# FFT mixing and a ReGLU layer on one core: compute only the distinct token columns, and store them in ranges of 16 or 32 rows

## The chip, the core and the metric

The kernel runs on one core of one Trainium2 chip. The core has five engines with instruction streams of their own: TensorE (PE in the profile, its weight loads as PEld), VectorE (DVE), ScalarE (ACT), GpSimd (POOL) and SyncE (SP), which here only issues DMAs. SBUF is the on-chip memory, PSUM the memory that matmuls write. The metric is the device time of one execution in microseconds; the time before is the median of nine runs.

## What is computed

For 8 batches of 3008 tokens with 256 features, the reference takes the real part of a two-dimensional FFT over tokens and features, and sends the result through a gated layer of width 1536:

```python
X = np.fft.fft(x, axis=1)          # x: (8, 3008, 256)
X = np.fft.fft(X, axis=2)
x = X.real.astype(np.float32).reshape(24064, 256)
gate = np.maximum(x @ w_gate, 0.0)
val = x @ w_val
out = (gate * val @ w_out).astype(np.float32)
```

The input is real. So the transform at token S-r is that of token r with the sign of one half of its parts turned. Tokens 1 to 1503 have a mirror at 1505 to 3007; tokens 0 and S/2 = 1504 are their own. That makes 1505 distinct token columns in a batch.

## The kernel before

The token transform is split as 94 x 32: a token is r = ka + 94*kb with ka from 0 to 93 and kb from 0 to 31. Only ka from 0 to 47 is computed, in three blocks (`blk` 0, 1, 2) of 512 columns. A block has four groups (g) of 128 columns, and a group has four runs (u) of 32: ka = 12*u + 4*blk + g, and kb runs inside. 3 x 512 = 1536 columns, 31 more than are distinct.

The start-up builds sine tables and folds the features' transform into the weights: `wc` and `ws` for the two parts, and `wm`, which is `ws` times -2 (its row 0 is zero). Then come 288 steps (8 batches x 3 blocks x 12 slices `f` of the width). In each step, on 512 columns:

- `gate` (L467): two matmuls into PSUM `G` (L473, L474), ACT's ReLU into `gs` (L475). In blocks 0 and 2 POOL sets 32 mirrored columns of `h` to zero (L480).
- `mirror_gate` (L482): one more matmul adds `wm` and turns `G` into the mirror's gate (L485); ACT's ReLU makes `gm` (L488). It is on 480 columns in blocks 0 and 2: those of ka = 0 and ka = 47 are left out, and the zeros stand for them.
- `value` (L490): two matmuls into `V` (L495, L497), and DVE multiplies `gs` and `V` into the direct half of `h` (L499).
- `mirror_value` (L515): in a split step DVE makes the mirror's value from `V` in two operations (`even` L505, then L519), and POOL multiplies it with `gm` into the mirrored half of `h` (L511). In an unsplit step a third matmul (L523) makes it instead. `split` (L463) is false for the first 18 steps, then in one of 6 steps up to step 48, and in one of 12 after that.

The mirrored half is written with kb reversed within each run of 32.

Twelve steps after a block's first step its output begins: `out_piece` (L534) is called twice a step and issues four matmuls each time (L546), `h` as the weights and `wo` with 256 columns streaming through, 12 to a group of 128 tokens. Two groups share a PSUM tile `po` (two of them take turns); ACT copies it to `os` (L555); `store` (L568) issues four DMAs of 32 rows, one for each u, on SP. In the last block's mirrored half each group is copied by DVE (L551) and stored at once by `store_last` (L559), with SP and ACT as issuers.

Between these steps a hand-written plan places the next batches' work: loading x and folding it (POOL), the transform's first stage (L164), a shuffle through DRAM (L182, L188), `rotate`, and the second stage, `stage2` (L199, matmuls at L206), which writes `pq`, whose imaginary row 0 goes through DRAM (`Nd`) and comes back in all partitions as `nb`. All the HBM transfers of this but the gather of `xh` are issued on SP, in the order of the plan, in one queue with the stores.

The order of each engine's instructions is fixed when the program is built. So are the completion counters (semaphores) of the DMAs of SP and ACT: there are eight, handed out in turn in the order in which the DMAs of both are placed, and a DMA waits until the one that had its counter before has landed.

Of the kernel before, what the change touches and what calls it, by code (L numbers as in the profile page):

```python
# [14 lines left out]
ALU = mybir.AluOpType  # L15
ACTF = mybir.ActivationFunctionType
# [27 lines left out]
def kernel(ctx: ExitStack, tc, x, w_gate, w_val, w_out, out):  # L44
# [154 lines left out]
    def stage2(b, blk, cs, evac):  # L199
        if cs == 0:  # L200
            pqt[b, blk] = pqp.tile([128, 2, 512], BF16, tag="pq", name="pq")
            nbt[b, blk] = pqp.tile([128, 512], BF16, tag="nb", name="nb")
        t4, pq = t4t[b], pqt[b, blk]
        ps = bank(b, "ps2")
        for g in range(4):
            nc.tensor.matmul(ps[:, g * 128:(g + 1) * 128], lhsT=t4[:, 4 * blk + g, cs * H:(cs + 1) * H],  # L206
                             rhs=m2[:, cs, :], start=True, stop=True)
        if evac == "act":
            nc.scalar.copy(pq[:, cs, :], ps[:])
        else:  # L210
# [73 lines left out]
    with tc.tile_pool(name="sp", bufs=1, space=SB) as sp:  # L284
        dve, pl = nc.vector, nc.gpsimd
# [31 lines left out]
        ps = psd.tile([128, 512], F32, tag="d", name="psk")  # L317
        for k in range(WARM):
# [4 lines left out]
                allow_small_or_imprecise_dtypes=True)  # L323

        def product(eng, lo, hi):
# [6 lines left out]
                allow_small_or_imprecise_dtypes=True)  # L332
# [47 lines left out]
        for blk in range(NBLK):  # L380
# [1 line left out]
        load_w(2)  # L382

        kbi = sp.tile([128, 4, NB], F32, tag="kbi")
        pl.iota(kbi[:], pattern=[[0, 4], [1, NB]], base=0, channel_multiplier=0, allow_small_or_imprecise_dtypes=True)
        ui = sp.tile([128, 4, NB], F32, tag="ui")
        pl.iota(ui[:], pattern=[[1, 4], [0, NB]], base=0, channel_multiplier=0, allow_small_or_imprecise_dtypes=True)
        di = sp.tile([128, 4, 2, 16], F32, tag="di")
# [1 line left out]
                allow_small_or_imprecise_dtypes=True)  # L390
# [64 lines left out]
    steps = [(b, blk, f) for b in range(B) for blk in range(NBLK) for f in range(NF)]  # L455
    ht = {}

    def mirrored(t):

        blk = steps[t][1]  # L460
        return slice(NB if blk == 0 else 0, 512 - NB if blk == NBLK - 1 else 512)

    def split(t):  # L463

        return 18 <= t < len(steps) and t % (6 if t < 48 else 12) != 5

    def gate(t):  # L467
        b, blk, f = steps[t]
        pq, fs = pqt[b, blk], slice(f * 128, (f + 1) * 128)
        e = ht[t] = {"h": hp.tile([128, 2, 512], BF16, tag="h", name="h"),  # L470
                     "G": psg.tile([128, 512], F32, tag="g", name="G"),
                     "gs": gp.tile([128, 512], F32, tag="gs", name="gs")}
        nc.tensor.matmul(e["G"][:], lhsT=wc[0][:, fs], rhs=pq[:, 0, :], start=True, stop=False)  # L473
        nc.tensor.matmul(e["G"][:], lhsT=ws[0][:, fs], rhs=pq[:, 1, :], start=False, stop=True)  # L474
        nc.scalar.activation(e["gs"][:], e["G"][:], ACTF.Relu)  # L475
        cols = mirrored(t)
        if cols.stop - cols.start < 512:

            lo = 0 if cols.start else cols.stop
            nc.gpsimd.memset(e["h"][:, 1, lo:lo + NB], 0.0)  # L480

    def mirror_gate(t):  # L482
        b, blk, f = steps[t]
        e, cols = ht[t], mirrored(t)
        nc.tensor.matmul(e["G"][:, cols], lhsT=wm[0][:, f * 128:(f + 1) * 128], rhs=pqt[b, blk][:, 1, cols],  # L485
                         start=False, stop=True, skip_group_check=True)
        e["gm"] = ep.tile([128, 512], F32, tag="gm", name="gm")
        nc.scalar.activation(e["gm"][:, cols], e["G"][:, cols], ACTF.Relu)  # L488

    def value(t, part):  # L490
        b, blk, f = steps[t]
        e, pq, fs = ht[t], pqt[b, blk], slice(f * 128, (f + 1) * 128)
        if part == 0:
            e["V"] = psv.tile([128, 512], F32, tag="v", name="V")
            nc.tensor.matmul(e["V"][:], lhsT=wc[1][:, fs], rhs=pq[:, 0, :], start=True, stop=split(t))  # L495
        else:
            nc.tensor.matmul(e["V"][:], lhsT=ws[1][:, fs], rhs=pq[:, 1, :], start=False, stop=True,  # L497
                             skip_group_check=split(t))
            nc.vector.tensor_tensor(e["h"][:, 0, :], e["gs"][:], e["V"][:], op=ALU.mult)  # L499

    def even(t):
        b, blk, f = steps[t]
# [5 lines left out]
    def mirror_h(t, eng, val):  # L508

        e, cols = ht[t], mirrored(t)  # L510
        eng.tensor_tensor(free(e["h"][:], 512 + cols.start + NB - 1, [NB, (cols.stop - cols.start) // NB], [-1, NB]),  # L511
                          e["gm"][:, cols].rearrange("p (a k) -> p a k", k=NB),
                          val[:, cols].rearrange("p (a k) -> p a k", k=NB), op=ALU.mult)

    def mirror_value(t):  # L515
        b, blk, f = steps[t]
# [17 lines left out]
    def out_piece(t, half):  # L534

        b, blk, f = steps[t]
        for k in range(8 * f + 4 * half, 8 * f + 4 * half + 4):
            gi, ff = divmod(k, NF)
            sg, s = divmod(gi, 4)
            g = 3 - s if sg else s  # L540
            if s == 0 and ff == 0:
                state["os"] = op.tile([128, 4, D], F32, tag="os", name="os")
            if s % 2 == 0 and ff == 0:
                state["po"] = pso.tile([128, 2, D], F32, tag="o", name="po")
            po, os_ = state["po"], state["os"]
            nc.tensor.matmul(po[:, s % 2, :], lhsT=ht[t - f + ff]["h"][:, sg, g * 128:(g + 1) * 128],  # L546
                             rhs=wo[:, ff, :], start=(ff == 0), stop=(ff == NF - 1))
            if ff < NF - 1:
                continue
            if t - f == len(steps) - NF and sg == 1:  # L550
                nc.vector.tensor_copy(os_[:, s:s + 1, :], po[:, s % 2:s % 2 + 1, :])  # L551
                store_last(b, blk, os_, s)
                continue
            if s % 2 == 1:
                nc.scalar.copy(os_[:, s - 1:s + 1, :], po[:])  # L555
            if s == 3:
                store(b, blk, sg, os_)

    def store_last(b, blk, os_, s):  # L559

        for u in range(4):
            ka = NKA * u + 4 * blk
            if s == 0 and ka + 3 == 47:
                continue
            (nc.sync if u % 2 or s < 2 else nc.scalar).dma_start(
                out=view(out, (b * S + NA - ka - 3 + s) * D, [[NA * D, NB], [1, D]]), in_=os_[32 * u:32 * u + 32, s, :])

    def store(b, blk, sg, os_):  # L568
        for u in range(4):
            ka = NKA * u + 4 * blk  # L570
            src = os_[32 * u:32 * u + 32].rearrange("p g d -> p (g d)")
            if sg == 0:
                nc.sync.dma_start(out=view(out, (b * S + ka) * D, [[NA * D, NB], [1, 4 * D]]), in_=src)
                continue

            lo = 1 if ka + 3 == 47 else 0
            hi = 3 if ka == 0 else 4
            row = b * S + NA - ka - 3 + lo
            nc.sync.dma_start(out=view(out, row * D, [[NA * D, NB], [1, (hi - lo) * D]]),
                              in_=src[:, lo * D:hi * D])  # L580

    extra = {}

# [29 lines left out]
    n = len(steps)  # L613
# [56 lines left out]
```

## Time and profile before

| | us |
|---|---|
| median of 9 runs (649.84 to 652.48) | 650.58 |
| the profiled execution | 650.94 |
| its span on the core | 649.2 |
| PE busy (4170 matmuls) | 625.5 |
| weight loads (PEld) | 408.6 |
| DVE busy | 565.9 |
| POOL busy | 509.1 |
| ACT busy | 425.0 |
| 192 POOL memsets of `h`, L480 | 22.8 |
| 94 output copies on ACT, L555 | 55.1 |

The costliest groups are the output matmuls (L546), POOL's mirror product (L511) and the seven operations of a step on ACT and DVE. The columns are: line, engine, operation, tiles and shapes, count; then busy us and mean ns of one; then idle us of the engine just before them, and who ended most of it.

```profile
L511 POOL TENSOR_TENSOR h<-gm,E 128x480 bf16<-128x480 f32 (+1 forms) x251 | 308.2, 1228 | 92.5 <-DVE E L519 66.7
L546 PE MATMUL po<-wo,h 128*128 128x256 bf16 x2304 | 337.2, 272 | 2.8 <-DVE os L551 1.1
L499 DVE TENSOR_TENSOR h<-gs,V 128x512 bf16<-128x512 f32 x288 | 195.8, 687 | 17.6 <-ACT gm L488 12.0
L475 ACT ACTIVATE gs<-G 128x512 f32<-128x512 f32 x288 | 171.5, 595 | 0.8 <-PE G L474 0.8
```

Such a mean is the time from an instruction's start to its end. Instructions overlap, so the distance between two starts can be shorter; busy time counts each moment once.

### The profile page before, as it was taken

The page shows a single profiled execution, that of the slowest core. Times are in us where ns is not written, and L with a number is a line of the kernel's source. Part 1 is how long each engine was busy: PE and PEld are TensorE (multiplying, and loading weights), DVE is VectorE, ACT ScalarE, POOL GpSimd, SP SyncE. Part 2 cuts the span into 40 slices and gives each one's busy share as a digit, 9 for nine tenths or more (in the row PEclk, how much of TensorE's full clock was granted, in tenths as well). Part 3 has the DMA queues.
Part 4 walks back from the last instruction along what each step waited for, and adds up shares of the span by engine and source line. Part 5 has one row for each costly group of instructions (what it writes and reads, how often), then busy time and mean ns, then how long its engine had stood idle before and what let it go on. Part 6 is the DMA issues. An engine that isn't in the chain of part 4 may idle for free.

```text
span 649.2 us, 12804 instructions
## 1 busy us (share of the span) xinstructions
PE 625.5 (96%) x4170; PEld 408.6 (63%) x4246; DVE 565.9 (87%) x889; ACT 425.0 (65%) x813; POOL 509.1 (78%) x716
## 2 busy tenths in 40 slices
PE   6888999999999999999999999999999999999995
PEld 3424666666666666666666666666666666666664
DVE  9857688889999998989989998998988988989991
ACT  5366676776666667676676666766666767766660
POOL 9649469968998699968998699967999666666660
PEclk9599999999999999999999999999999999999999
DMA  9792473295134651295324852285322142212113
GB/s 246 226 229 50 126 192 82 58 217 177 40 82 115 148 161 42 50 188 156 81 66 112 175 142 60 50 172 149 102 50 73 31 131 73 50 34 64 32 40 88
DMA packets 32823, 70.77 MB, mean 109 GB/s; under 512 B 4650, under 2 KB 22146, under 8 KB 30754
## 3 DMA queue, kind: packets, MB, share of 16 engines
q1 hardware_dynamic: 30228, 58.03, 34.2%
q0 software_dynamic: 2336, 11.80, 9.0%
q8 instruction: 33, 0.54, 0.4%
q14 instruction: 34, 0.28, 0.1%
q10 hardware_dynamic: 192, 0.13, 0.1%
HBM read 39.77 MB, written 30.96 MB: 109 GB/s over the span
## 4 chain that ended last, share of the span: by engine, by line
PE 87%; DVE 5%; POOL 4%; issue 2%; ACT 1%; DVEq 0%; POOLq 0%; ACTq 0%
PE po L546 38%; PE V L497 9%; PE G L474 9%; PE G L485 8%; PE V L495 8%; PE G L473 8%; PE ps L164 2%; POOL eo L132 2%; DVE E L505 2%; PE ps L206 2%; PE psw L263 2%; DVE h L499 1%; PE V L523 1%; DVE E L519 1%; POOL h L511 1%
## 5 line engine op out<-in xcount | busy, mean ns | idle before, releaser
L511 POOL TENSOR_TENSOR h<-gm,E 128x480 bf16<-128x480 f32 (+1 forms) x251 | 308.2, 1228 | 92.5 <-DVE E L519 66.7
L546 PE MATMUL po<-wo,h 128*128 128x256 bf16 x2304 | 337.2, 272 | 2.8 <-DVE os L551 1.1
L546 PEld LDWEIGHTS <-h 128*128 128x128 bf16 x2304 | 222.8, 98 | 90.9 <-issue 2.8
L488 ACT ACTIVATE gm<-G 128x480 f32<-128x480 f32 (+1 forms) x288 | 167.5, 582 | 126.7 <-PE G L485 113.3
L499 DVE TENSOR_TENSOR h<-gs,V 128x512 bf16<-128x512 f32 x288 | 195.8, 687 | 17.6 <-ACT gm L488 12.0
L505 DVE SCALAR_TENSOR_TENSOR E<-nb,af,V 128x480 f32<-128x480 bf16 (+1 forms) x245 | 177.7, 725 | 22.4 <-PE V L495 12.4
L475 ACT ACTIVATE gs<-G 128x512 f32<-128x512 f32 x288 | 171.5, 595 | 0.8 <-PE G L474 0.8
L519 DVE SCALAR_TENSOR_TENSOR E<-E,V 128x480 f32<-128x480 f32 (+1 forms) x245 | 161.3, 658 | 0.0
L497 PE MATMUL V<-pq,ws 128*128 128x512 bf16 x287 | 108.7, 379 | 1.6 <-DVE E L505 1.1
L485 PE MATMUL G<-pq,wm 128*128 128x480 bf16 (+1 forms) x288 | 106.7, 370 | 2.2 <-ACT gs L475 2.2
L474 PE MATMUL G<-pq,ws 128*128 128x512 bf16 x281 | 106.5, 379 | 2.2 <-DVE pq L211 0.4
L495 PE MATMUL V<-pq,wc 128*128 128x512 bf16 x255 | 96.6, 379 | 0.0
L473 PE MATMUL G<-pq,wc 128*128 128x512 bf16 x253 | 95.9, 379 | 0.1
L555 ACT COPY os<-po 128x512 f32<-128x512 f32 x94 | 55.1, 586 | 60.2 <-PE po L546 60.2
L104 POOL TENSOR_TENSOR eo<-xl 94x254 bf16<-94x254 f32 (+2 forms) x100 | 74.7, 751 | 0.4
L101 POOL TENSOR_TENSOR xl<-xl,xh 94x510 f32<-94x510 f32 (+2 forms) x50 | 66.0, 1319 | 3.9
L497 PEld LDWEIGHTS <-ws 128*128 128x128 bf16 x288 | 28.2, 98 | 33.7
L474 PEld LDWEIGHTS <-ws 128*128 128x128 bf16 x288 | 28.2, 98 | 31.5 <-issue 0.2
L511 DVE TENSOR_TENSOR h<-gm,V 128x480 bf16<-128x480 f32 (+1 forms) x37 | 24.6, 665 | 22.7 <-ACT gm L488 17.1
L174 ACT CAST t<-ps 96x512 bf16<-96x512 f32 x63 | 36.9, 585 | 5.8 <-PE ps L162 5.4
L495 PEld LDWEIGHTS <-wc 128*128 128x128 bf16 x288 | 28.1, 98 | 10.5 <-issue 3.7
L485 PEld LDWEIGHTS <-wm 128*128 128x128 bf16 x288 | 28.2, 98 | 7.6 <-issue 4.1
(108 smaller groups left out, 349.1 us busy)
## 6 DMA issues: line engine op xcount, KB each, us to landing
out_dram<-os SPq DMA_DIRECT2D x173, 128.0 KB
xl<-in_x_dram SPq DMA_DIRECT2D x7, 1360.0 KB
Td<-t SPq DMA_DIRECT2D x7, 768.0 KB
t<-Td SPq DMA_DIRECT2D x7, 768.0 KB
nb<-Nd SPq DMA_DIRECT2D x24, 128.0 KB
xl<-in_x_dram SPq DMA_DIRECT2D x7, 238.0 KB
xl<-in_x_dram SPq DMA_DIRECT2D x4, 384.0 KB
xh<-in_x_dram SPq DMA_DIRECT2D x4, 384.0 KB
```

The source lines that it names most:

```text
L473: nc.tensor.matmul(e["G"][:], lhsT=wc[0][:, fs], rhs=pq[:, 0, :], start=True, stop=False)
L474: nc.tensor.matmul(e["G"][:], lhsT=ws[0][:, fs], rhs=pq[:, 1, :], start=False, stop=True)
L475: nc.scalar.activation(e["gs"][:], e["G"][:], ACTF.Relu)
L485: nc.tensor.matmul(e["G"][:, cols], lhsT=wm[0][:, f * 128:(f + 1) * 128], rhs=pqt[b, blk][:, 1, cols], start=False, stop=True, skip_group_ ...
L488: nc.scalar.activation(e["gm"][:, cols], e["G"][:, cols], ACTF.Relu)
L495: nc.tensor.matmul(e["V"][:], lhsT=wc[1][:, fs], rhs=pq[:, 0, :], start=True, stop=split(t))
L497: nc.tensor.matmul(e["V"][:], lhsT=ws[1][:, fs], rhs=pq[:, 1, :], start=False, stop=True, skip_group_check=split(t))
L499: nc.vector.tensor_tensor(e["h"][:, 0, :], e["gs"][:], e["V"][:], op=ALU.mult)
L505: nc.vector.scalar_tensor_tensor(e["E"][:, cols], nbt[b, blk][:, cols], af[:, f:f + 1], e["V"][:, cols], op0=ALU.mult, op1=ALU.add)
L511: eng.tensor_tensor(free(e["h"][:], 512 + cols.start + NB - 1, [NB, (cols.stop - cols.start) // NB], [-1, NB]), e["gm"][:, cols].rearrange ...
L519: nc.vector.scalar_tensor_tensor(e["E"][:, cols], e["E"][:, cols], 2.0, e["V"][:, cols], op0=ALU.mult, op1=ALU.subtract)
L546: nc.tensor.matmul(po[:, s % 2, :], lhsT=ht[t - f + ff]["h"][:, sg, g * 128:(g + 1) * 128], rhs=wo[:, ff, :], start=(ff == 0), stop=(ff == ...
```

## The change

`mirrored` and the new `direct` set the columns. In block 0 the first 16 columns fall away, in block 2 the last 15 or 16: direct products run on 496, 512 and 497 columns in the three blocks, mirrored ones on 496, 512 and 496. The run ka = 0 is turned by half (the iota `kbi` starts at NB/2 there), so that what falls away lies at the block's edge. Column 496 of the third block is token S/2, made by one extra one-column matmul in `stage2` for each half.

The mirrored half of `h` is now written fully reversed from its first column on, both halves begin at column 0, and the zeroing memset is gone. The last output group of an edge block therefore has 113 or 112 tokens (`m`), and its copy on ACT is done group by group.

`store` works out from `rows` which rows of `os` belong to consecutive output rows, and issues one DMA for each such range: 16 or 32 rows, with one of 15 rows in block 0 and the single row of token S/2. The very last half is stored group by group in the same way, each group with a `po` of its own; in its last group SP and ACT take turns. `store_last` is gone. `value` takes the columns of `direct` in the same way as `gate` in the diff, for both matmuls and the product.

```diff
@@ stage2
+        if blk == NBLK - 1:
+            nc.tensor.matmul(ps[:, 496:497], lhsT=t4[:, 0, cs * H:(cs + 1) * H], rhs=m2[:, cs, 0:1], start=True, stop=True)
@@ tables
-        pl.iota(kbi[:], pattern=[[0, 4], [1, NB]], base=0, channel_multiplier=0, allow_small_or_imprecise_dtypes=True)
+        pl.iota(kbi[:, 0, :], pattern=[[1, NB]], base=NB // 2, channel_multiplier=0,
+                allow_small_or_imprecise_dtypes=True)
+        pl.iota(kbi[:, 1:4, :], pattern=[[0, 3], [1, NB]], base=0, channel_multiplier=0, allow_small_or_imprecise_dtypes=True)
@@ columns
+    LO, HI = NB // 2, 512 - NB // 2
     def mirrored(t):
-        return slice(NB if blk == 0 else 0, 512 - NB if blk == NBLK - 1 else 512)
+        return slice(LO if blk == 0 else 0, HI if blk == NBLK - 1 else 512)
+    def direct(t):
+        return slice(LO if blk == 0 else 0, HI + 1 if blk == NBLK - 1 else 512)
@@ gate
-        nc.tensor.matmul(e["G"][:], lhsT=wc[0][:, fs], rhs=pq[:, 0, :], start=True, stop=False)
-        nc.tensor.matmul(e["G"][:], lhsT=ws[0][:, fs], rhs=pq[:, 1, :], start=False, stop=True)
-        nc.scalar.activation(e["gs"][:], e["G"][:], ACTF.Relu)
-        cols = mirrored(t)
-        if cols.stop - cols.start < 512:
-            lo = 0 if cols.start else cols.stop
-            nc.gpsimd.memset(e["h"][:, 1, lo:lo + NB], 0.0)
+        ds = direct(t)
+        nc.tensor.matmul(e["G"][:, ds], lhsT=wc[0][:, fs], rhs=pq[:, 0, ds], start=True, stop=False)
+        nc.tensor.matmul(e["G"][:, ds], lhsT=ws[0][:, fs], rhs=pq[:, 1, ds], start=False, stop=True)
+        nc.scalar.activation(e["gs"][:, ds], e["G"][:, ds], ACTF.Relu)
@@ mirror_h
-        eng.tensor_tensor(free(e["h"][:], 512 + cols.start + NB - 1, [NB, (cols.stop - cols.start) // NB], [-1, NB]),
-                          e["gm"][:, cols].rearrange("p (a k) -> p a k", k=NB),
-                          val[:, cols].rearrange("p (a k) -> p a k", k=NB), op=ALU.mult)
+        n = cols.stop - cols.start
+        eng.tensor_tensor(free(e["h"][:], 512 + n - 1, [-1, n]), e["gm"][:, cols], val[:, cols], op=ALU.mult)
@@ out_piece
-            if s % 2 == 0 and ff == 0:
+            if (g % 2 == 0 or last) and ff == 0:
                 state["po"] = pso.tile([128, 2, D], F32, tag="o", name="po")
-            nc.tensor.matmul(po[:, s % 2, :], lhsT=ht[t - f + ff]["h"][:, sg, g * 128:(g + 1) * 128],
+            nc.tensor.matmul(po[0:m, i, :], lhsT=ht[t - f + ff]["h"][:, sg, g * 128:g * 128 + m],
                              rhs=wo[:, ff, :], start=(ff == 0), stop=(ff == NF - 1))
-            if t - f == len(steps) - NF and sg == 1:
-                nc.vector.tensor_copy(os_[:, s:s + 1, :], po[:, s % 2:s % 2 + 1, :])
-                store_last(b, blk, os_, s)
+            if last:
+                nc.vector.tensor_copy(os_[0:m, g:g + 1, :], po[0:m, 0:1, :])
+                store(b, blk, sg, os_, g, g + 1, (nc.sync, nc.scalar) if g == 3 else (nc.sync,))
                 continue
-            if s % 2 == 1:
-                nc.scalar.copy(os_[:, s - 1:s + 1, :], po[:])
-            if s == 3:
-                store(b, blk, sg, os_)
+            if m < 128:
+                nc.scalar.copy(os_[:, g - 1, :], po[:, 0, :])
+                nc.scalar.copy(os_[0:m, g, :], po[0:m, 1, :])
+            elif g % 2 == 1:
+                nc.scalar.copy(os_[:, g - 1:g + 1, :], po[:])
+            if g == 3:
+                store(b, blk, sg, os_, 0, 4, (nc.sync,))
@@ store
+        for k, (p, n, ga, ng, ra) in enumerate(parts):
+            queues[k % len(queues)].dma_start(
+                out=view(out, ra * D, [[NA * D, n], [1, ng * D]]),
+                in_=os_[p:p + n, ga:ga + ng, :].rearrange("p g d -> p (g d)"))
+        if blk == NBLK - 1 and sg == 0:
+            nc.sync.dma_start(out=view(out, (b * S + S // 2) * D, [[D, 1], [1, D]]), in_=os_[HI % 128:HI % 128 + 1, 3, :])
```

In the built programs SP issues 199 stores before and 287 after, ACT 4 and 2. The last group alone has 15 before (11 on SP) and 23 after (21 on SP).

More of the change, by code (lines that the diff above doesn't have):

```diff
@@ L456 @@
     ht = {}
+    LO, HI = NB // 2, 512 - NB // 2
     def mirrored(t):
         blk = steps[t][1]
-        return slice(NB if blk == 0 else 0, 512 - NB if blk == NBLK - 1 else 512)
+        return slice(LO if blk == 0 else 0, HI if blk == NBLK - 1 else 512)
+    def direct(t):
+        blk = steps[t][1]
+        return slice(LO if blk == 0 else 0, HI + 1 if blk == NBLK - 1 else 512)
     def split(t):
@@ L492, in value @@
         e, pq, fs = ht[t], pqt[b, blk], slice(f * 128, (f + 1) * 128)
+        ds = direct(t)
         if part == 0:
             e["V"] = psv.tile([128, 512], F32, tag="v", name="V")
-            nc.tensor.matmul(e["V"][:], lhsT=wc[1][:, fs], rhs=pq[:, 0, :], start=True, stop=split(t))
+            nc.tensor.matmul(e["V"][:, ds], lhsT=wc[1][:, fs], rhs=pq[:, 0, ds], start=True, stop=split(t))
         else:
-            nc.tensor.matmul(e["V"][:], lhsT=ws[1][:, fs], rhs=pq[:, 1, :], start=False, stop=True,
+            nc.tensor.matmul(e["V"][:, ds], lhsT=ws[1][:, fs], rhs=pq[:, 1, ds], start=False, stop=True,
                              skip_group_check=split(t))
-            nc.vector.tensor_tensor(e["h"][:, 0, :], e["gs"][:], e["V"][:], op=ALU.mult)
+            nc.vector.tensor_tensor(e["h"][:, 0, 0:ds.stop - ds.start], e["gs"][:, ds], e["V"][:, ds], op=ALU.mult)
     def even(t):
@@ L538, in out_piece @@
             gi, ff = divmod(k, NF)
-            sg, s = divmod(gi, 4)
-            g = 3 - s if sg else s
-            if s == 0 and ff == 0:
+            sg, g = divmod(gi, 4)
+            last = t - f == len(steps) - NF and sg == 1
+            cs = (mirrored if sg else direct)(t - f)
+            m = min(128, cs.stop - cs.start - 128 * g)
+            if g == 0 and ff == 0:
                 state["os"] = op.tile([128, 4, D], F32, tag="os", name="os")
-            if s % 2 == 0 and ff == 0:
+            if (g % 2 == 0 or last) and ff == 0:
                 state["po"] = pso.tile([128, 2, D], F32, tag="o", name="po")
             po, os_ = state["po"], state["os"]
-            nc.tensor.matmul(po[:, s % 2, :], lhsT=ht[t - f + ff]["h"][:, sg, g * 128:(g + 1) * 128],
+            i = 0 if last else g % 2
+            nc.tensor.matmul(po[0:m, i, :], lhsT=ht[t - f + ff]["h"][:, sg, g * 128:g * 128 + m],
                              rhs=wo[:, ff, :], start=(ff == 0), stop=(ff == NF - 1))
@@ L556, in out_piece @@
-            if s == 3:
-                store(b, blk, sg, os_)
[L559 to L563, printed above, removed]
-                continue
[L565 to L573, printed above, removed]
-                continue
[L576 to L580, printed above, removed]
+            if m < 128:
[3 more added lines that the diff above has]
+                nc.scalar.copy(os_[:, g - 1:g + 1, :], po[:])
@@ new lines, in out_piece, with rows @@
+            if g == 3:
+                store(b, blk, sg, os_, 0, 4, (nc.sync,))
+    def rows(b, blk, sg):
+        ds = (direct, mirrored)[sg]((b * NBLK + blk) * NF)
+        for c in range(512):
+            if not ds.start <= c < ds.stop:
+                continue
+            g, u, k = c // 128, c // 32 % 4, c % 32
+            ka, kb = NKA * u + 4 * blk + g, (k + NB // 2) % NB if u == 0 else k
+            r = ka + NA * kb
+            if sg and r in (0, S // 2) or ka == NKA * 4 - 1 and kb == NB // 2:
+                continue
+            p = ds.stop - 1 - c if sg else c - ds.start
+            yield p % 128, p // 128, b * S + (S - r if sg else r)
@@ new lines, in store @@
+    def store(b, blk, sg, os_, g0, g1, queues):
+        runs = {}
+        for p, g, r in rows(b, blk, sg):
+            if g0 <= g < g1:
+                runs.setdefault(p, []).append((g, r))
+        parts = []
+        for p in sorted(runs):
+            (ga, ra), n = min(runs[p]), len(runs[p])
+            assert sorted(runs[p]) == [(ga + i, ra + i) for i in range(n)]
+            if parts and parts[-1][0] + parts[-1][1] == p and parts[-1][2:4] == (ga, n) and \
+                    parts[-1][4] + NA * parts[-1][1] == ra:
+                parts[-1] = (parts[-1][0], parts[-1][1] + 1) + parts[-1][2:]
+            else:
+                parts.append((p, 1, ga, n, ra))
+        for k in range(len(parts) - 1):
+            (p, n, ga, ng, ra), (p1, n1, ga1, ng1, r1) = parts[k:k + 2]
+            if (n + n1) % 16 == 0 and n % 16 and ga == ga1 and ng > ng1 and r1 == ra + NA * n:
+                parts[k:k + 2] = [(p, n + n1, ga, ng1, ra), (p, n, ga + ng1, ng - ng1, ra + ng1)]
+        for k, (p, n, ga, ng, ra) in enumerate(parts):
[4 more added lines that the diff above has]
+            nc.sync.dma_start(out=view(out, (b * S + S // 2) * D, [[D, 1], [1, D]]), in_=os_[HI % 128:HI % 128 + 1, 3, :])
```

## The prediction

> **What bounds the kernel now.** I read the page first (busy shares, then the chain that ended last), then one stretch of the windows, then the timeline of one step for the price of a matmul, then the last 14 us, because stores leave there.
>
> ```profile
> PE 625.5 (96%) x4170; PEld 408.6 (63%) x4246; DVE 565.9 (87%) x889; ACT 425.0 (65%) x813; POOL 509.1 (78%) x716
> PE 87%; DVE 5%; POOL 4%; issue 2%; ACT 1%; DVEq 0%; POOLq 0%; ACTq 0%
> 240.00:320.00 80.00, 79.42 (x549) 53.42 (x559) 74.44 (x118) 54.74 (x107) 71.18 (x102) 1.00 0.46 111
> ```
>
> TensorE carries 87% of the chain, and in the middle stretch (engine columns PE, PEld, DVE, ACT, POOL, then clock, DMA share, GB/s) it is busy 79.42 of 80 us at full clock. DVE has 5.6 us free there, POOL 8.8. So the middle is priced in matmul columns. A matmul's printed duration (370 to 379 ns) is its latency; its price is the distance between starts:
>
> ```profile
> 251.36 0.37 PE L485 MATMUL G<-pq,wm 128*128 128x480 bf16 x1
> 251.56 0.38 PE L473 MATMUL G<-pq,wc 128*128 128x512 bf16 x1
> 251.77 0.38 PE L474 MATMUL G<-pq,ws 128*128 128x512 bf16 x1
> 251.99 0.37 PE L523 MATMUL V<-pq,wm 128*128 128x480 bf16 x1
> ...
> 317.61 0.18 PE L194 MATMUL psr<-t,rot 128*128 128x12 bf16 x1
> 317.64 0.49 PE L546 MATMUL po<-wo,h 128*128 128x256 bf16 x3
> ```
>
> 512 columns hold the array 216 ns (251.56 to 251.99 for two), 480 columns 0.20 us: 0.42 ns a column. The 12-column matmul holds it 0.03 us, far more than twelve columns are worth.
>
> ```profile
> 637.57 1.72 SPq L573 DMA_DIRECT2D out_dram<-os  x4
> 638.80 2.78 PE L546 MATMUL po<-wo,h 128*128 128x256 bf16 x24 [0.57 <-DVE os L551]
> 639.39 7.35 SPq L565 DMA_DIRECT2D out_dram<-os  x11
> 642.08 2.83 ACTq L565 DMA_DIRECT2D out_dram<-os  x4
> 642.10 1.47 PE L546 MATMUL po<-wo,h 128*128 128x256 bf16 x12 [0.51 <-DVE os L551]
> 643.61 0.42 DVE L551 COPY os<-po 128x256 f32<-128x256 f32 x1 [1.56 <-PE po L546]
> ...
> 643.63 3.11 SPq L565 DMA_DIRECT2D out_dram<-os  x7
> ...
> SPq L565 <- DMA out_dram<-os: 2.4, 1, 2.4
> ```
>
> The last copy ends at 644.03, yet the span ends at 649.17: 5.14 us in which SP still issues stores (3.11/7 = 0.44 us each), the last one starting at 646.32, then its landing and the closing barrier. The last line is from SP's own waits: once in the tail SP stood 2.4 us until a store had landed. In the order of the built program the stores take eight completion counters in turn, and a store waits for the one eight places earlier. ACT's two stores of piece 2 stand, in that turn, before SP's second store of piece 1; SP therefore waited from about 641.2 until ACT's store (issued 642.08, after the third copy) had landed at 643.63: 1.55 us from issue to landing.
>
> **What the skill says.** "TensorE: Matmul & The Clock Gate", section Back-to-back issue gap: a warm gap of N/2.4 + 2.5 ns with a floor near 25 ns for few columns; the trace agrees (216 ns at 512, 29 ns for the 12-column one). The same page, Weight-path perf modes, says that fast weight loading is on only for 128 weights; pieces of 112 or 113 tokens lose it. The trace agrees in kind: 98 ns for a 128-column load (L546), about 122 ns for the 96-column ones of L164. "DMA: Bandwidth & Descriptors", Issuing engines are not separate DMA queues: issuing from several engines saves only issue time; here issue time (0.44 us a store) is what the tail consists of.
>
> **The change part by part**, against the profiled execution: span 649.17, time 650.94; the median of the nine runs is 0.36 lower.
>
> 1. Columns. In blocks 0 and 2 the direct matmuls go from 512 to 496 or 497, the mirrored ones from 480 to 496. A split step has four direct (L473, L474, L495, L497) and one mirrored matmul: block 0 saves 64 - 16 = 48 columns, block 2 60 - 16 = 44. Unsplit steps have a second mirrored one (L523): 32 and 28. By `split` block 0 has 76 split and 20 unsplit steps, block 2 87 and 9. Columns: 76x48 + 20x32 + 87x44 + 9x28 = 8,368, at 0.4215 ns (216/512) = -3.53 us. The output matmuls (L546) stream 256 columns of wo whatever the number of tokens: nothing saved on 2,304 of them.
> 2. One column more in stage 2: 16 matmuls, at the 29 ns of the 12-column row: +0.46 us. Above, if the weight load shows, 98 ns: 1.6; below, nothing is gained.
> 3. Slow weight loads: two short pieces in each of 16 edge blocks, 12 loads each = 384. In stage 1 a 256-column matmul before a 96-column load took 113 ns instead of 109; with 127 columns before it none showed. So 0 to 4 ns, I take 2: +0.77 us (0 to 1.5).
> 4. DVE: in an edge step h loses 15 or 16 columns, E gains 16 twice. One column costs about 1.03 ns (714 against 747 ns at 480 and 512): +17 ns, some 0.5 us in the 80 us stretch, inside its 5.6 us. Per split step DVE's closest starts add to about 1.87 us then, PE's to 1.92. If that cover were gone, the gain of item 1 would go with it.
> 5. POOL loses 192 memsets (22.8 us) and gains 16 columns in the edge steps (1205 to 1274 ns for 32 columns, so +35 ns each, some 5.7 us). Nothing on the chain waits for POOL after the start-up. ACT: gs and gm exchange 16 columns; 31 output copies of 586 ns become two of about half, some 60 to 100 ns more each; behind them on ACT stands the next gm, which mostly waits for PE anyway (113 us in all). Cost nil. The split iota: POOL is not late there; nil.
> 6. Stores in the middle. SP issues 287 stores instead of 199, 88 x 0.44 = 39 us more of a queue that waits over 300 us for output copies. Behind them stand the Nd/nb loads, the x loads and the shuffle, in the same order as before; they come at most two or three issues, about 1.3 us, later, and their users are two or more steps (4 us) away. Nil, up to +1.
> 7. The last group's matmuls. Each piece now takes its own `po`, so the 0.57 and 0.51 us in which PE waited for a copy go: -1.08.
> 8. The last stores. A piece now leaves in 6, 6, 6 and 5 ranges, 23 issues instead of 15, 21 of them on SP. And in the built order ACT's two stores of the very last piece take counters 6 and 7 before SP's fourth and fifth store of the *first* piece. SP's fourth store thus waits for the last copy, ACT's issue and its landing. Behind it on SP stand 18 stores (3 + 6 + 6 + 3). With Tc the end of the last copy: first at Tc + 0.03 + 1.55, the second 0.47 later (the other ACT store), 16 more at 0.44, so the last starts at Tc + 9.1. From there the old tail applies (649.17 - 646.32 = 2.85). End: Tc + 11.9 instead of Tc + 5.14: +6.8. Unknown: whether 16 rows issue cheaper than 32. A one-row store (Nd) takes 228 ns, but loads of 80, 96 and 128 rows take 0.33 to 0.43 as 32 do, so rows hardly matter. At 0.36 (the shortest distance seen) it is +5.5, at 0.47 +7.3.
>
> Sum: -3.53 + 0.46 + 0.77 - 1.08 + 6.8 = +3.4. Own time 654.3; against the median, **654.0**.
>
> **Rivals.**
> *Little left over, about 651.9.* Item 3 at zero, items 1 and 7 in full, issues at 0.36 us: -3.53 + 0.46 - 1.08 + 5.5 = +1.35, just at the bound of what can be told from no change. For it: shorter distances exist in the trace. Against: seven issues in a row took 3.11 us.
> *The columns bring nothing, about 656.3.* If DVE ends last in edge steps, item 1's net 2.3 us vanishes, or late nb rows cost as much. For it: DVE is busy 93% and its h, E, E rows stand in the chain in the last batch. Against: PE idles 0.6 us in 80. Sum -1.1 + 6.8 = +5.7.
> *Faster, about 645.5.* One mechanism: SP does not stand behind ACT's last stores (the counters bind differently from the listed order) and 16-row issues cost like the one-row 0.23. Then SP keeps pace and only three issues follow the last copy: last start Tc + 0.6 instead of Tc + 2.3, so -2.3 - 1.1 - 1.7 = -5.1. Without the wait but at 0.44 us, SP would reach its last store near 647 and end about 1 us later than now; so it decides below about 0.35 us an issue. Against: SP's 2.4 us wait in the old tail is this very mechanism.
>
> **How the numbers follow.** Likeliest, 0.63: 654.0, own range 652.4 to 655.6 (items 2, 3 and 8 at their ends). Columns bring nothing: 0.15. Little left over: 0.16. Faster: 0.06. The range for 8 in 10: 651.6 to 656.2, which takes in most of both neighbours. A measurement of this kernel tells about 0.2% (1.3 us) from no change; of the case that lies at this bound I put 0.10 inside. Faster 0.06, same 0.10, slower 0.84.
>
> **What would show it.** Steps: starts of the edge steps' matmuls 209 ns apart, a 12-step block with 496 columns about 0.24 us shorter, PE still the chain until the tail. Short-piece loads: L556 starts 109 or 113 ns apart. Tail: no PE wait on `os`; SP's waits with one entry of over 2 us on a store, 18 SP stores in a row after the last copy, over some 8 us; span's end about 12 us after the last DVE copy. It would be wrong if SP issues steadily before the last copy, if 16-row stores issue in about 0.2 us, or if PE gets idle time in edge steps.

## The result, and the profile after

| | before | after |
|---|---|---|
| median, us | 650.58 (31 runs, 648.98 to 652.48) | 654.6 (10 runs, 652.62 to 656.92) |
| the profiled execution | 650.94 | 656.45 |
| its span | 649.17 | 654.68 |

The ratio is 1.0064, with an interval of 1.0052 to 1.0076: slower by about 4 us. The page after, its row of busy times and the first line of its chain:

```profile
PE 626.0 (96%) x4231; PEld 414.7 (63%) x4262; DVE 563.7 (86%) x889; ACT 427.3 (65%) x844; POOL 502.7 (77%) x525
PE 75%; DVE 10%; POOL 6%; DMA 4%; issue 2%; ACT 1%; SPq 1%; POOLq 0%; DVEq 0%; ACTq 0%
```

POOL and DVE have less to do, as the change means them to. But TensorE's share of the chain fell from 87% to 75%, and DMA, which had no entry, now has 4%. So something other than TensorE ended stretches in the middle of the kernel. The end shows first. This is the timeline of the last 14 us after (start, length, engine, line, operation, tiles, count; in brackets the idle time before it and who ended that):

```profile
636.74 5.73 PE L556 MATMUL po<-wo,h 128*113 128x256 bf16 x51
...
641.00 11.68 SPq L606 DMA_DIRECT2D out_dram<-os  x21
...
642.51 0.42 DVE L561 COPY os<-po 112x256 f32<-112x256 f32 x1 [0.89 <-PE po L556]
...
642.97 0.85 ACTq L606 DMA_DIRECT2D out_dram<-os  x2
```

The output matmuls now run in one piece of 51 with no wait on `os`: the two gaps of before are gone. The last copy ends at 642.93, the span at 654.68, which is 11.75 us later; before it was 5.14. The same stretch in SP's own timeline from 643.5 on, and the entry of SP's waits after (waited for; us, times, longest) that stands before it:

```profile
644.49 8.19 SPq L606 DMA_DIRECT2D out_dram<-os  x18
```

```profile
SPq L606 <- DMA out_dram<-os: 2.2, 1, 2.2
```

SP stood 2.2 us until ACT's store of the last group had landed, then issued 18 stores in 8.19 us, 0.455 us each.

Now the middle. The windows view of 240 to 320 us after (us, then busy us and count of PE, PEld, DVE, ACT, POOL, then clock, DMA share, GB/s):

```profile
240.00:320.00 80.00, 78.98 (x554) 53.79 (x557) 73.65 (x117) 54.70 (x109) 70.08 (x77) 1.00 0.44 110
```

TensorE is busy for 78.98 us here, 79.42 before: less work, yet also more idle time. Where it stood is in the waits of all engines after:

```profile
POOL eo L99 <- DMA xl<-in_x_dram: 14.5, 5, 3.6
...
PE V L505 <- DVE E L513: 3.3, 10, 0.6
...
DVE E L513 <- POOL h L520: 3.0, 6, 0.7
...
POOL eo L99 <- DMA xh<-in_x_dram,ix: 2.3, 1, 2.3
```

and one such stop in the timeline of 244 to 246 us after:

```profile
243.58 1.27 POOL L520 TENSOR_TENSOR h<-gm,E 128x512 bf16<-128x512 f32 x1
...
244.88 0.73 DVE L513 SCALAR_TENSOR_TENSOR E<-nb,af,V 128x496 f32<-128x496 bf16 x1 [0.65 <-POOL h L520]
...
245.66 0.37 PE L505 MATMUL V<-pq,ws 128*128 128x497 bf16 x1 [0.60 <-DVE E L513]
```

Read it backwards. PE's second value matmul waits for DVE's first operation on E, because that one still reads the first product in `V`, to which this matmul will add. DVE waits for POOL's product of an earlier step: `E` and `gm` have four buffers, and POOL has not yet read the oldest. PE stands 0.60 us. DVE waits for POOL like this six times, in the third to the sixth batch and at the same two steps of a batch. The same wait existed before, three times with 0.6 us in all.

POOL is busy only 77% over the kernel, but not evenly: from 223.55 to 278.7 us, while it folds the next x, its timeline has no idle gap above 0.1 us (before from 223.37 to 279.2). In that stretch a late start can't be made up. It became late some 20 us before the stop. SP's timeline of 196 to 236 us, after:

```profile
201.94 2.64 SPq L606 DMA_DIRECT2D out_dram<-os  x6
204.62 0.28 SPq L610 DMA_DIRECT2D out_dram<-os  x1
205.00 0.78 SPq L83 DMA_DIRECT2D xl<-in_x_dram  x2
```

and before:

```profile
202.75 1.71 SPq L573 DMA_DIRECT2D out_dram<-os  x4
204.56 0.84 SPq L83 DMA_DIRECT2D xl<-in_x_dram  x2
```

Before, four stores stand ahead of the load of x (1.71 us), now seven (3 us). The load's issue moved only from 204.56 to 205.00, but the steps are some 0.6 us ahead by then, so against the work it serves the load is about a microsecond later. POOL's timeline of the first operation that needs x, after:

```profile
223.55 0.22 POOL L99 TENSOR_TENSOR eo<-xl,xh 94x4 bf16<-94x4 f32 x1 [3.60 <-DMA xl<-in_x_dram]
```

and before:

```profile
223.37 0.22 POOL L99 TENSOR_TENSOR eo<-xl,xh 94x4 bf16<-94x4 f32 x1 [2.44 <-DMA xh<-in_x_dram,ix]
```

POOL waited here before as well, 2.44 us for the gathered `xh`; now it waits 3.60 us for `xl`. Its next products of `h` queue behind this, and the delay stays with it until the fold is done. The chain of the work that ended last, followed back from the stop of 245.66 us (start, length, what), leads over DVE, POOL, the load of x and the stores to an output copy:

```profile
201.53 0.39 ACT os L566
...
201.94 0.32 SPq L606
...
205.37 18.02 DMA xl<-in_x_dram
...
243.62 1.24 POOL h L520
...
245.66 0.37 PE V L505
```

Where the 5.51 us between the two spans lie, with the steps of both traces set side by side:

| part | us |
|---|---|
| start-up, to the first `gs` (37.18 and 36.96) | -0.22 |
| body of 8 batches (592.52 and 593.07) | +0.55 |
| last steps, to the end of the last copy | -1.43 |
| after the last copy | +6.61 |

The body is nearly even, and the question is how much it hides.

### The profile page after: what moved, and what is told of

Read it like the earlier page. It is cut to its first block, busy times and chain, and to the rows that moved or that the text cites. A ratio compares the mean times of both kernels' runs of the same rounds, so it can differ in the third digit from the quotient of the medians.

```text
span 654.7 us, 12850 instructions
## 1 busy us (share of the span) xinstructions
PE 626.0 (96%) x4231; PEld 414.7 (63%) x4262; DVE 563.7 (86%) x889; ACT 427.3 (65%) x844; POOL 502.7 (77%) x525
## 4 chain that ended last, share of the span: by engine, by line
PE 75%; DVE 10%; POOL 6%; DMA 4%; issue 2%; ACT 1%; SPq 1%; POOLq 0%; DVEq 0%; ACTq 0%
PE po L556 31%; PE V L505 8%; PE G L486 8%; PE G L492 7%; PE V L503 7%; PE G L485 7%; DMA xl<-in_x_dram 4%; DVE E L513 3%; POOL h L520 3%; DVE h L507 2%; PE ps L206 2%; PE psw L265 2%; PE ps L164 2%; DVE E L526 2%; PE V L530 1%
## 5 line engine op out<-in xcount | busy, mean ns | idle before, releaser
L520 POOL TENSOR_TENSOR h<-gm,E 128x496 bf16<-128x496 f32 (+1 forms) x251 | 312.8, 1248 | 91.2 <-DVE E L526 72.9
L556 PE MATMUL po<-wo,h 128*128 128x256 bf16 (+2 forms) x2304 | 336.8, 272 | 0.5
L556 PEld LDWEIGHTS <-h 128*128 128x128 bf16 (+2 forms) x2304 | 229.7, 103 | 83.3 <-issue 2.9
L495 ACT ACTIVATE gm<-G 128x496 f32<-128x496 f32 (+1 forms) x288 | 170.3, 591 | 126.2 <-PE G L492 113.6
L507 DVE TENSOR_TENSOR h<-gs,V 128x497 bf16<-128x497 f32 (+2 forms) x288 | 193.0, 678 | 16.0 <-ACT gm L495 10.0
L513 DVE SCALAR_TENSOR_TENSOR E<-nb,af,V 128x496 f32<-128x496 bf16 (+1 forms) x245 | 180.3, 736 | 25.1 <-PE V L503 19.9
L487 ACT ACTIVATE gs<-G 128x497 f32<-128x497 f32 (+2 forms) x288 | 169.7, 589 | 0.8 <-PE G L486 0.8
L526 DVE SCALAR_TENSOR_TENSOR E<-E,V 128x496 f32<-128x496 f32 (+1 forms) x245 | 164.0, 669 | 0.0
L505 PE MATMUL V<-pq,ws 128*128 128x497 bf16 (+2 forms) x288 | 107.9, 374 | 3.5 <-DVE E L513 3.3
L492 PE MATMUL G<-pq,wm 128*128 128x496 bf16 (+1 forms) x288 | 107.9, 375 | 2.3 <-ACT gs L487 2.2
```

What stands on the lines that cost most here:

```text
L487: nc.scalar.activation(e["gs"][:, ds], e["G"][:, ds], ACTF.Relu)
L505: nc.tensor.matmul(e["V"][:, ds], lhsT=ws[1][:, fs], rhs=pq[:, 1, ds], start=False, stop=True, skip_group_check=split(t))
L507: nc.vector.tensor_tensor(e["h"][:, 0, 0:ds.stop - ds.start], e["gs"][:, ds], e["V"][:, ds], op=ALU.mult)
L513: nc.vector.scalar_tensor_tensor(e["E"][:, cols], nbt[b, blk][:, cols], af[:, f:f + 1], e["V"][:, cols], op0=ALU.mult, op1=ALU.add)
L520: eng.tensor_tensor(free(e["h"][:], 512 + n - 1, [-1, n]), e["gm"][:, cols], val[:, cols], op=ALU.mult)
L526: nc.vector.scalar_tensor_tensor(e["E"][:, cols], e["E"][:, cols], 2.0, e["V"][:, cols], op0=ALU.mult, op1=ALU.subtract)
```

## The experiments

The runs tell three things apart: whether the tail is a wait or a number of issues; whether the gaps in the middle come from POOL's lag, and this from the number of stores; and whether the columns pay at all. All nine kernels compute the whole result. The kernel before was measured again beside them, with medians of 650.46 (runs 1 to 4), 650.31 (5 to 8) and 650.47 (9), and the ratios refer to it. Where a run is compared with the change's 654.6, or with a run of another group, differences of some 0.3 us mean nothing.

**1. The last group on SP alone.**

```diff
-                store(b, blk, sg, os_, g, g + 1, (nc.sync, nc.scalar) if g == 3 else (nc.sync,))
+                store(b, blk, sg, os_, g, g + 1, (nc.sync,))
```

> The changed kernel with all 23 stores of the last group on SP, none on ACT. My theory: SP no longer stands 2.2 us before its fourth store; from its third store (641.82 in the profile of the change) 20 more follow at 0.46 us, the last starts near 651.0 instead of 652.26, so the time falls by about 1.3 us, to 653.3 median; 8 us of SP stores still follow the last copy, because their number is the larger part of the tail's cost. Rival: the wait behind ACT's stores is the whole of the tail's cost; then the time falls by 6 us or more, below 649. Second rival: the tail does not set the end; then it stays at 654.6.

Measured: 653.6, ratio 1.0044 [1.0028, 1.0059]. In the timeline of its last microseconds:

```profile
640.70 10.50 SPq L606 DMA_DIRECT2D out_dram<-os  x23
...
642.22 0.42 DVE L561 COPY os<-po 112x256 f32<-112x256 f32 x1 [0.89 <-PE po L556]
```

The wait is gone, and SP issues all 23 stores in one row: it starts before the last copy and still needs until 651.2. Only 1.0 us comes back, since ACT's two stores are now SP's. The tail is made of issues; the wait adds little.

**2. Six buffers of E and of gm instead of four.**

```diff
-    ep = ctx.enter_context(tc.tile_pool(name="ep", bufs=4, space=SB))
+    ep = ctx.enter_context(tc.tile_pool(name="ep", bufs=6, space=SB))
```

> The changed kernel with six E and six gm buffers instead of four. My theory: POOL lags as before (up to 9 us behind gs), POOL's wait for x stays, but DVE's E (L513) no longer waits for POOL, the PE gaps of 0.6 to 1.0 us go, and the time falls by 2 to 3 us, to about 652. Rival: PE's gaps come from something else that is late with x or the shuffle (t4, pq, nb); then the gaps and the 654.6 stay.

Measured: 651.06 (650.64 to 651.94), ratio 1.0001 [0.999, 1.0013]: 3.5 us less than the change. Its waits keep one such entry:

```profile
DVE E L513 <- POOL h L520: 0.2, 1, 0.2
```

The six waits of up to 0.7 us are one of 0.2. POOL still waits for x as long as in the change (17.2 us for `xl` and `xh` without one wait of 11.6 us in the start-up, against 16.8); it may be late now without stopping DVE. The runs also lie closer together, 1.3 us from end to end instead of 4.3.

**3. The old kernel with more stores.** If the number of issues on SP makes POOL late, it must do so without any change of columns. So in the kernel before, the direct half of the third block leaves in eight stores of 16 rows instead of four of 32, in the first seven batches:

```diff
-                nc.sync.dma_start(out=view(out, (b * S + ka) * D, [[NA * D, NB], [1, 4 * D]]), in_=src)
+                for k in (0, 16) if blk == NBLK - 1 and b < B - 1 else (0,):
+                    n = 16 if blk == NBLK - 1 and b < B - 1 else NB
+                    nc.sync.dma_start(out=view(out, (b * S + ka + k * NA) * D, [[NA * D, n], [1, 4 * D]]),
+                                      in_=src[k:k + n])
```

> The kernel before, with the four 32-row stores of block 2's direct half issued as eight stores of 16 rows in the first seven batches; columns, products and the tail are untouched. My theory: SP reaches the x loads about 1.8 us later minus the time it waited there for POOL anyway (1.7 us in three of the batches), so POOL's wait for x and its lag grow by some 1 us as in the change: gaps of 0.3 to 1 us, 1 to 3 us in all, about 652.5. Rival: more store issues in the middle are hidden as my prediction said, and the stalls belong to the new columns or products; then 650.6.

Measured: 652.17, ratio 1.003 [1.0022, 1.0038]. The same stop appears in its timeline, in the old kernel's lines:

```profile
320.06 0.71 DVE L505 SCALAR_TENSOR_TENSOR E<-nb,af,V 128x480 f32<-128x480 bf16 x1 [0.63 <-POOL h L511]
...
320.83 0.38 PE L497 MATMUL V<-pq,ws 128*128 128x512 bf16 x1 [0.56 <-DVE E L505]
```

It comes once in each of four batches, the third to the sixth, where PE's start is 0.78, 0.94, 0.59 and 0.67 us after the one before instead of 0.22. (The gaps of 0.6 to 1.0 us in the expectations of runs 2 and 4 are such distances between starts too.) Four more issues ahead of the load of x are enough; neither the columns nor the reversed writing is needed.

**4. The load of x two steps earlier** (one step in the first batch). The gather stays in its place; the two SP loads move ahead of the stores.

```diff
-            at(t0 + tl, load_x, b + 2, nc.sync)
+            at(t0 + (17 if b == 0 else 5), load_x, b + 2, nc.sync, 0)
+            at(t0 + tl, load_x, b + 2, nc.sync, 1)
```

> The changed kernel with the two SP loads of the next x (L83) issued before the direct stores of block 2 instead of after them; the gather on POOL stays where it was. My theory: in the change seven or eight stores stand before these loads, x lands about 1 us later in the step count, POOL's first fold operation waits for it, POOL falls further behind, and the four E and gm buffers run out near steps 23 to 26 of a batch, so that DVE and then PE wait (six gaps of 0.6 to 1.0 us). Then the time falls by 2 to 3 us, to about 652, and the six gaps are gone. Rival: POOL falls behind because its fully reversed product or PE's quicker pace is too much for it; then the gaps stay and the time stays at 654.6.

Measured: 656.01, ratio 1.0076 [1.0057, 1.0095], slower than the change by 1.4. Of the six waits of DVE for POOL's product one of 0.2 us is left (eight of 0.2 us for its fold remain), as an earlier load would have it. But a new stop appears in the second batch. SP's timeline from 130 us on, and the timeline of 144 to 153 us:

```profile
130.87 0.78 SPq L84 DMA_DIRECT2D xl<-in_x_dram  x2
131.74 2.76 SPq L610 DMA_DIRECT2D out_dram<-os  x6
```

```profile
150.20 0.59 ACT L572 COPY os<-po 128x512 f32<-128x512 f32 x1 [4.29 <-DMA out_dram<-os]
...
151.83 0.59 PE L496 MATMUL G<-pq,wm 128*128 128x512 bf16 x1 [3.40 <-ACT gs L491]
```

Six stores of the direct half are issued right behind the load, the last by 134.5 us, and ACT's next copy into their `os` waits until they have landed, which is at 150.2: some 16 us, where stores of these sizes land in 1.9 to 2.3 us in the median of run 2. So the copy waits 4.29 us, `gs` behind it is late, and PE stands for 3.40 us. The windows of this kernel just after it:

```profile
152.00:155.00 3.00, 3.00 (x11) 1.51 (x10) 0.69 (x1) 1.19 (x2) 2.69 (x4) 0.50 0.68 208
```

The clock was granted at 0.50 for these 3 us. That block of 12 steps took 29.99 us instead of 24.81. The time missed its expectation; the later batches (73.2 to 73.8 us each, 73.5 to 74.9 in the change) agree with it. Issued behind the large load, and beside POOL's gather from 132.2 us on, the stores landed late, and so the buffer that they free came late.

**5. The kernel before with six buffers.** Edit 2, on before.

> The kernel before with six E and six gm buffers instead of four. My theory: POOL's lag already touched the four buffers now and then in the kernel before (gaps of 0.16 to 0.35 us at three places, PE excess of 3.2 us in all against 1.9 us in the changed kernel with six), so it gains 1 to 2 us, about 649. Then most of what six buffers gave the changed kernel (3.5 us) was the change's own stall. Rival: the kernel before gains the same 3.5 us, to 647; then the buffers have nothing to do with the change.

Measured: 648.37, ratio 0.9977 [0.9969, 0.9984], 1.9 us less than before. So of the 3.5 us of run 2 about 1.9 belong to both kernels and about 1.6 to the change's own stalls. In the profiled executions the body of eight batches is 1.35 us shorter with six buffers (591.17 against 592.52). Which of the old kernel's waits give this is not settled: its three waits of DVE for POOL sum to 0.6 us.

**6. Six buffers, and SP and ACT in turn for all four last groups.**

```diff
-                store(b, blk, sg, os_, g, g + 1, (nc.sync, nc.scalar) if g == 3 else (nc.sync,))
+                store(b, blk, sg, os_, g, g + 1, (nc.sync, nc.scalar))
```

> The changed kernel with six E and gm buffers, and SP and ACT taking turns in all four of the last stores. Theory (counters in turn): ACT's stores of pieces 2, 3 and 4 stand in the turn before SP's of piece 1, so SP waits once for the third copy's ACT store and once for the fourth's; from the latter's landing (1.58 us after the last copy) only 8 stores follow at 0.46, the last starts 5.0 us after the last copy instead of 9.3: 4.3 us less than with six buffers alone, about 646.8. Rival (only the number of stores an engine issues counts): SP and ACT have 12 and 11, both are done about 2.5 us after the last copy, about 644.3.

Measured: 648.61, ratio 0.9976 [0.9965, 0.9987]; the gain came, less than expected. Its timeline of the end:

```profile
633.80 5.77 SPq L606 DMA_DIRECT2D out_dram<-os  x5
634.59 6.19 ACTq L606 DMA_DIRECT2D out_dram<-os  x11
...
638.01 0.42 DVE L561 COPY os<-po 112x256 f32<-112x256 f32 x1 [0.89 <-PE po L556]
...
640.28 5.43 SPq L606 DMA_DIRECT2D out_dram<-os  x12
```

SP has half the issues, but five stores of the direct half spread over 5.77 us, held by the landings of ACT's; 12 stores were left at 640.28, where I had counted on 8. With the counters shared in turn, two issuing engines did not halve the tail here: the last store still starts 6.9 us after the last copy.

**7. Six buffers, and one store for the four last groups.** The last half is stored after its last copy, in 6 ranges of four groups each:

```diff
-                store(b, blk, sg, os_, g, g + 1, (nc.sync, nc.scalar) if g == 3 else (nc.sync,))
+                if g == 3:
+                    store(b, blk, sg, os_, 0, 4, (nc.sync,))
```

> The changed kernel with six E and gm buffers, and the last half stored at once after its fourth copy, all on SP: 6 stores with up to four rows of 1 KB each instead of 23. Theory: SP is free when the last copy ends, the last store starts 2.3 us after it instead of 9.3 and lands about 0.4 us later for its larger size: 6.5 us less than with six buffers alone, about 644.6, faster than the kernel before. Rival (the end is set by landing or by the closing barrier, not by SP's issues): under 2 us less, about 649.5.

Measured: **644.36**, ratio 0.9913 [0.9898, 0.9928]: 10.2 us below the change and about 6 below the kernel before, the fastest of all. Its end, in the timeline:

```profile
636.68 0.43 DVE L561 COPY os<-po 112x256 f32<-112x256 f32 x1 [0.89 <-PE po L556]
...
637.13 2.64 SPq L607 DMA_DIRECT2D out_dram<-os  x6
```

Six stores in 2.64 us, and the span ends at 642.1, 5.0 us after the last copy. In the windows of 240 to 320 us PE is full again:

```profile
240.00:320.00 80.00, 79.85 (x567) 54.44 (x566) 73.76 (x117) 55.79 (x111) 70.75 (x78) 1.00 0.43 106
```

**8. The kernel before with both edits.** Six buffers, and its last half stored at once in place of `store_last`. This is run 7 without the columns and without the separate `po`.

```diff
-                store_last(b, blk, os_, s)
+                if s == 3:
+                    store(b, blk, sg, os_)
```

> The kernel before with six E and gm buffers and with its last half stored at once on SP (4 stores of 32 rows instead of 15). Theory: the last store starts 1.4 us after the last copy instead of 2.3 and lands 0.4 us later: about 0.5 us less than with six buffers alone, about 648.4. Against this kernel the changed one with the same two edits should lead by its columns (3.1 us) and its separate po tiles (1.1 us) less two more stores (0.9 us): about 3.3 us. Rival: the columns save nothing once both are free of stalls; then the two are within 1 us.

Measured: 647.3, ratio 0.9962 [0.9948, 0.9976]. Run 7 is 2.9 us faster on the same chip: with the stalls and the tail out of the way, columns and `po` do pay.

**9. The change with only the last store's edit**, four buffers as it was:

> The changed kernel with its four E and gm buffers as they are, and only the last half stored at once on SP (6 stores instead of 23). Theory: the tail's cost and the stalls from POOL's lag add up without touching each other, so this takes off what it took off with six buffers (651.06 - 644.36 = 6.7 us): about 647.9. Rival: part of the tail's gain in that run came through the buffers (fewer stalls in the last batch, a steadier clock); then clearly less than 6 us comes off and the time stays above 649.

Measured: 647.66, ratio 0.9959 [0.9947, 0.9971]. This fills the square of the two edits on the change (medians, us):

| | stores group by group | one store at the end |
|---|---|---|
| four buffers | 654.6 | 647.66 |
| six buffers | 651.06 | 644.36 |

6.9 and 6.7 across, 3.5 and 3.3 down: the gains of the two edits add and don't cover one another.

## Why the prediction was right, and where it was not

It gave 654.0 and +3.4; measured were 654.6 and +4.0. By its steps:

**Item 1 (columns, -3.53) and item 2 (+0.46): right in size.** In the edge steps matmuls of 496 and 497 columns start 209 to 210 ns apart. The extra one-column matmul, in the view of its line after (duration min, median, max; first and last start):

```profile
L209 PE MATMUL ps<-m,t x16: 167/167/167, 60.4 to 561.4; 128*128 128x1 bf16 x16
```

167 ns is latency; the distance to the next start is 28 to 29 ns. Compared without stalls, run 7 against run 5, the body of eight batches is 588.71 against 591.17 us: -2.45, where -3.07 was predicted. A later batch takes 73.47 instead of 73.85, -0.38, which is an eighth of -3.07. The first two batches gain only 0.12 each, and why they gain less is open.

**Item 3 (slow weight loads, +0.77): wrong, it is nothing.** The groups after, with forms kept apart (busy us, mean ns):

```profile
L556 PEld LDWEIGHTS <-h 128*128 128x128 bf16 x1920 | 184.9, 98 | 73.9 <-issue 2.5
...
L556 PEld LDWEIGHTS <-h 128*112 128x112 bf16 x288 | 33.8, 130 | 7.6 <-issue 0.4
```

The load of 112 columns takes 130 ns instead of 98. The Trainium skill ("TensorE: Matmul & The Clock Gate", Weight-path perf modes) says that only 128 weights load fast, and the trace agrees. But the matmuls still start 109 ns apart: the longer load is hidden beside the matmuls before it. The 113 against 109 ns that I had taken from stage 1 didn't carry over.

**Items 4 and 5 (DVE, POOL and ACT): right as amounts of work.** DVE's busy time is 563.7 (565.9 before), POOL's 502.7 (509.1), ACT's 427.3 (425.0), and in run 7 PE is busy 79.85 of 80 us with the same columns. But item 5 also said that nothing on the chain waits for POOL after the start-up. That was not so even before; a piece of the chain before, from the second batch, with DVE's `E` between the two:

```profile
169.72 1.25 POOL h L511
...
171.76 0.38 PE V L497
```

**Item 6 (stores in the middle, nil, up to +1): this is the step whose mechanism failed.** It said that the loads behind the stores come some 1.3 us later and that "their users are two or more steps (4 us) away". The lateness was right. But the first operation of the fold stood in POOL's queue waiting for x before the change already; the waits of all engines before show it, a view that the prediction did not use:

```profile
POOL eo L99 <- DMA xh<-in_x_dram,ix: 10.6, 5, 2.5
```

A user that already waits has no distance. Behind it stand POOL's products, which free the four `E` and `gm` buffers, and thus DVE and PE. Runs 2 and 3 show the two halves of it: more stores alone make the stop, and more buffers remove it. Its price is about 1.6 us at the medians (run 2 against run 5), above the +1 that item 6 allowed. In the profiled execution, which was 1.9 us above its median, it was 3.0: the body's +0.55 against -2.45. The stops account for it: at the six after, PE's start comes later than its usual distance by 3.5 us in sum, at the one of 171.76 us before by 0.5.

**Item 7 (`po`, -1.08): right in mechanism, too small.** Both gaps (0.57 and 0.51) are gone, and up to the end of the last copy 1.43 us were gained. The last 96 output matmuls begin like this in PE's timeline before:

```profile
631.52 6.71 PE L546 MATMUL po<-wo,h 128*128 128x256 bf16 x60
```

The pieces of 24 and 12 that follow stand in the prediction's lines. The same 96 after:

```profile
631.83 10.64 PE L556 MATMUL po<-wo,h 128*128 128x256 bf16 x96
```

They took 12.05 us (631.52 to 643.57) and now take 10.64, 1.41 less. The printed idle time counts from the printed end of a matmul, 272 ns after its start, while matmuls in a row start 109 ns apart. So each gap cost 0.16 us more than is printed; the prediction, which priced matmuls by their starts, took the gaps as printed.

**Item 8 (the last stores, +6.8): right, in mechanism and size.** The last store starts 9.32 us after the last copy (9.1 predicted), the span ends 11.75 after it (11.9), with one SP wait of 2.2 us and 18 stores in a row. 16 rows cost as much as 32: the median distance between issues in a row is 0.463 us with both. The weight of the two parts I had not separated: run 1 shows that without the wait nearly all of it stays.

Of the rivals, "the columns bring nothing" was wrong (run 7 against run 8), and "faster" fell with SP's wait and 0.46 us an issue. "Little left over" had items 3 and 7 right and the issue time wrong. That the total came so close is in part luck. The columns brought 0.62 us less than items 1 and 2 say, and item 3's cost of 0.77 did not come, which nearly cancels. Item 6's stalls, some 1.6 us that were counted as nil, stand against 0.35 more from item 7 and 0.2 less in item 8.

The Trainium skill ("DMA: Bandwidth & Descriptors", Issuing engines are not separate DMA queues) calls the time to initiate a DMA usually small relative to the DMA itself. In this tail it is the larger part: 18 x 0.455 us against one landing of 1.55.

## What to carry to other kernels

Count a store by its issue and not by its bytes: splitting an output into more ranges lengthens its queue by 0.46 us a range here, and at the end of this kernel every issue after the last copy was paid in full. A last half stored at once in six issues beat one stored early in 23. Before calling a delayed transfer hidden, look whether its first user already waits for it and what is queued behind that user; a buffer or two more then may be worth more than a better place for the load, as here (run 2 against run 4). And price an idle gap of TensorE by the distance between starts, not by the idle time printed.

## What the runs showed of the hardware that was not expected

- A longer stop of TensorE cost more than itself: after 3.4 us idle, the clock was granted at 0.50 for the next 3 us (run 4).
- The clock in the start-up differs from one execution to the next. The windows of 28 to 37 us, in the profile of before:

```profile
28.00:37.00 9.00, 8.01 (x31) 3.21 (x33) 5.22 (x16) 5.84 (x12) 5.48 (x5) 0.78 1.07 304
```

and in that of run 5, whose instructions there are the same:

```profile
28.00:37.00 9.00, 8.43 (x39) 3.25 (x40) 5.65 (x18) 5.81 (x12) 6.02 (x6) 1.00 1.11 308
```

At 0.78 the first `gs` comes at 37.18 us, at 1.00 at 35.5. The eleven profiles fall into these two groups: six with 0.75 to 0.80 in this window have the first `gs` at 36.8 to 37.5 us, five with 1.00 at 35.5 to 36.0. Two profiled spans can thus differ by 1 to 2 us before the first step; that is why the parts above are measured from there. The medians contain the start-up, so a difference like the 1.6 us of item 6 is rough.
